# Two phases per 512 tokens in the mlp, and row maxima in visits of six banks, in a gated attention and mlp kernel

## The chip, the cores and the metric

The kernel runs on one core of a Trainium2 chip. The metric is the device time of one execution in microseconds (us), lower is better. The time of the kernel before is the median of three runs; the profile is of one further execution.

## What is computed

For 2048 tokens of width 448, a multi-head attention (16 heads of 28) and an mlp (pre-layernorm, 1792 hidden units, tanh gelu) are mixed by a gate per token. All is fp32.

```python
x = A_x                                              # [1, 2048, 448]
g = sigmoid((x * gate_w).sum(-1, keepdims=True))
q, k, v = split(x @ wqkv)                            # 16 heads of 28
a = softmax(q @ k.T * 28 ** -0.5) @ v                # per head
a = a.reshape(1, 2048, 448) @ wo
y = layernorm(x)                                     # over 448
b = gelu(y @ w1 + b1) @ w2 + b2                      # 448 -> 1792 -> 448
return g * a + (1 - g) * b
```

## The kernel before

**Split operands.** TensorE multiplies in fp32r, a rounded form of fp32. To keep the accuracy every operand is split in a rounded part (names with h: `w1h`, `yh`, `hh`, `khi`) and the rest (names with l: `w1l`, `yl`, `hl`, `klo`), and a product is the sum of three matmuls: high by high, high by low, low by high. The rounded part is written by ScalarE (`activation(..., Copy)`), the rest by a subtraction on GpSimd (POOL in the profile) or VectorE (DVE). The 448 rows of a contraction are four tiles of 128; the last holds 64 rows twice, high and low, and takes two matmuls. So a product over 448 takes 11 matmuls.

**Three stages, in order of the program.**

1. The projection (`qk_tile`, `v_tile`). For each chunk `c` of 512 tokens there are seven tiles of q and k, stored in DRAM as high and low part (`qk`), and four tiles of v with the gate's sum (`vs`). Eight PSUM banks are used in turn (`next_ps`). Beside it run the statistics of layernorm: `ln_stats` in chunk 1, `ln_rows` and `ln_turn` in chunk 2 (means and inverse deviations are transposed and stored as rows in `lns`), and the first layernorm, `ln_load` and `ln_apply`, in chunks 2 and 3. The weights of the first two column blocks are loaded in chunk 2 (`load_w`).

2. The mlp. The hidden units are 14 column blocks `f` of 128. `mlp1(c, f)` computes one block for 512 tokens in one PSUM bank, bank 0, with 11 matmuls (L419). ScalarE empties it twice with the gelu, once rounded (`hh`, L424) and once whole (`h`, L425), and GpSimd makes `hl` (L426). `mlp2(c, f)` adds the block's part to the output of four token tiles in banks 4 to 7, with three matmuls each (L432, L433, L435). The loop runs `mlp1` of a step and then `mlp2` of the step before, so 56 steps. At a chunk's end the four banks are copied (ScalarE; in the last chunk VectorE, L443) and stored in `gbs`. In the first chunk each step loads and splits the weights of the block after next: `load_w` with two staging buffers for w1 and two for w2. Layernorm of the next chunk (`ln_apply`, mostly on GpSimd) runs in steps 6 to 12 of a chunk, on double-buffered `yh`, `yl`.

3. The attention. 64 score units per 512 queries of four heads, five units at a time: three row-group matmuls per unit (L591), exponentials on ScalarE (L596), the product with v (L620), and every 512 queries a normalisation and the output projection (`finish`, `project`), added to the gated mlp output `acc`.

**Row maxima.** The softmax subtracts an approximate row maximum, taken over the product of the high parts of q and k alone. It is 64 matmuls for each of 16 groups of 512 queries and four heads (each contracts 28 rows in one of four row groups of the array, L313), a reduction on VectorE (L293 for one bank, L295 for two) and one closing transpose, 1040 items in all. The class `RowMax` makes them and `Filler` spreads them: in the mlp `filler.run` counts slots (one per mlp matmul) and, when at least `MG` items are due, makes a visit of `MG` matmuls in the banks from 1 on. `MLP_MAX` = 476 items are made in the mlp, from step `FS` on, and the rest in the attention.

```python
if self.max is not None and self.due(n) >= min(MG, self.upto - self.done) > 0:
    self.max.issue(1, min(MG, self.upto - self.done))
```

**Order.** TensorE's instructions stand in the order of the program in all stages. In the projection and the mlp the order on the other queues (ScalarE, VectorE, GpSimd, and SP, which issues the DMAs) comes from a scheduler; in the attention they too stand in program order. Each queue works strictly in its order.

## Time and profile before

| | |
|---|---|
| median of three runs | 1266.08 us (1265.72 to 1268.47) |
| profiled execution | 1261.53 us |
| its span, first to last instruction | 1259.7 us |
| mean granted TensorE clock | 0.981 |
| TensorE matmul busy | 1188.8 us (94%) |
| VectorE / ScalarE / GpSimd busy | 770.1 / 633.2 / 335.2 us |

How to read the rows in the next section. A row of stretches has the stretch, its length, then busy time and number of instructions of PE (TensorE matmul), PEld (its weight loads), DVE, ACT (ScalarE) and POOL, the granted clock (1.00 is full), the busy share of the DMA engines and GB/s. A row of groups has the line, engine, operation, output and inputs with shapes, the count, then busy us and mean ns of one, then the idle time of the engine just before them with what ended it. A row of a timeline has start, duration, engine, line and operation, and in brackets the idle time before it and what ended it. Matmuls are pipelined, so the durations of neighbours overlap.

### The profile page before, as it was taken

What the parts mean: (1) busy time and instruction counts of PE and PEld (TensorE: products, weight loads), DVE (VectorE), ACT (ScalarE), POOL (GpSimd) and SP (SyncE); (2) the same over time, 40 slices, a digit from 0 to 9 for tenths busy, and PEclk for the clock granted to TensorE, in tenths of its full rate; (3) what the DMA queues carried; (4) which work ended last, traced back from release to release, by engine and by line L of the source; (5) the groups of instructions that cost most, each with busy time, mean ns of one, the idle gap of its engine ahead of it and who ended that gap; (6) DMA issues with size and microseconds to landing.
All of it is one profiled execution on the core that took longest, in us unless ns stands there. A gap on an engine that the chain in (4) does not pass through costs nothing.

```text
span 1259.7 us, 19889 instructions
## 1 busy us (share of the span) xinstructions
PE 1188.8 (94%) x8133; PEld 690.9 (55%) x8133; DVE 770.1 (61%) x1118; ACT 633.2 (50%) x663; POOL 335.2 (27%) x361
## 2 busy tenths in 40 slices
PE   7998679899999999979999999999999999999997
PEld 5887556566666666654444444444444444444443
DVE  3543047677777777766666666666667666666503
ACT  5333531211222121227766776677667667766774
POOL 4014881611221111114424521122022202201220
PEclk9999889999999999989999999999999999999998
DMA  8986661200010000036310022010102100001001
GB/s 263 307 292 202 182 168 37 71 8 1 9 62 8 8 30 8 1 95 158 95 54 17 18 54 57 14 29 25 45 18 59 33 16 18 25 2 54 25 25 60
DMA packets 52328, 83.44 MB, mean 66 GB/s; under 512 B 8268, under 2 KB 28252, under 8 KB 51324
## 3 DMA queue, kind: packets, MB, share of 16 engines
q1 hardware_dynamic: 48044, 76.04, 20.1%
q0 software_dynamic: 4192, 6.12, 1.9%
q8 instruction: 64, 1.05, 0.4%
q14 instruction: 28, 0.23, 0.1%
HBM read 55.49 MB, written 26.49 MB: 65 GB/s over the span
## 4 chain that ended last, share of the span: by engine, by line
PE 80%; DMA 7%; POOL 5%; DVE 4%; issue 2%; SPq 1%; ACT 1%; DVEq 0%; POOLq 0%; ACTq 0%
PE bank L620 19%; PE bank L591 18%; PE bank L313 17%; PE bank L419 10%; PE bank L435 4%; PE bank L432 3%; PE bank L433 3%; PE bank L506 2%; DMA xraw<-in_xt 2%; DVE acc L509 2%; POOL vg L119 1%; PE bank L508 1%; PE bank L507 1%; POOL vg L118 1%; DMA r<-in_w 1%
## 5 line engine op out<-in xcount | busy, mean ns | idle before, releaser
L596 ACT ACTIVATE pt<-bank 128x1536 f32<-128x1536 f32 (+1 forms) x410 | 484.7, 1234 | 208.5 <-PE bank L591 208.5
L293 DVE TENSOR_REDUCE mx<-bank 128x1 f32<-128x512 f32 x712 | 473.0, 686 | 153.0 <-PE bank L313 143.4
L313 PE MATMUL bank<-khi,qd 28*128 28x512 f32 x1024 | 364.7, 490 | 29.1 <-DVE acc L509 20.8
L313 PEld LDWEIGHTS bank<-khi,qd 28*128 28x128 f32 x1024 | 143.5, 183 | 235.6 <-DVE mx L293 114.9
L620 PE MATMUL bank<-pt,vg 128*32 128x512 f32 x2048 | 262.9, 604 | 0.0
L295 DVE TENSOR_REDUCE mx<-bank 128x2 f32<-128x1024 f32 x156 | 190.9, 1224 | 114.5 <-PE bank L313 114.2
L591 PE MATMUL bank<-qh,khi 29*128 29x512 f32 x1024 | 218.2, 476 | 0.0
L424 ACT ACTIVATE hh<-bank,b1s 128x512 fp32r<-128x512 f32 x56 | 38.4, 686 | 295.8 <-PE bank L419 295.8
L591 PE MATMUL bank<-qh,klo 28*128 28x512 f32 x1024 | 184.7, 397 | 0.0
L591 PE MATMUL bank<-ql,khi 28*128 28x512 f32 x1024 | 180.9, 390 | 0.0
L419 PE MATMUL bank<-yh,w1f 128*128 128x512 f32 x448 | 153.2, 414 | 11.9 <-ACT h L425 11.9
L426 POOL TENSOR_TENSOR hl<-h,hh 128x512 fp32r<-128x512 f32 x56 | 71.8, 1283 | 281.4 <-ACT h L425 262.4
L509 DVE SCALAR_TENSOR_TENSOR acc<-bank,gate,acc 128x448 f32<-128x448 f32 x64 | 43.7, 684 | 105.7 <-PE bank L508 104.2
L591 PEld LDWEIGHTS bank<-qh,khi 29*128 29x128 f32 x1024 | 87.1, 183 | 37.7 <-ACT pt L596 32.3
L419 PEld LDWEIGHTS bank<-yh,w1f 128*128 128x128 f32 x448 | 83.4, 191 | 41.4 <-issue 14.4
L435 PE MATMUL bank<-w2h,hl 128*128 128x448 f32 x224 | 89.4, 399 | 14.0 <-POOL hl L426 14.0
L591 PEld LDWEIGHTS bank<-ql,khi 28*128 28x128 f32 x1024 | 94.2, 187 | 15.1
L591 PEld LDWEIGHTS bank<-qh,klo 28*128 28x128 f32 x1024 | 92.1, 186 | 5.3
L620 PEld LDWEIGHTS bank<-pt,vg 128*32 128x32 f32 x2048 | 45.8, 109 | 84.0 <-issue 83.2
L519 POOL DMA_DIRECT2D lt<-ob x15 | 10.8, 720 | 301.6 <-DVE ob L518 301.6
L432 PE MATMUL bank<-w2h,hh 128*128 128x448 f32 x224 | 86.4, 386 | 0.0
L433 PE MATMUL bank<-w2l,hh 128*128 128x448 f32 x224 | 82.9, 370 | 0.0
(97 smaller groups left out, 1097.2 us busy)
## 6 DMA issues: line engine op xcount, KB each, us to landing
qk<-hl SPq DMA_DIRECT2D x28, 512.0 KB
xraw<-in_xt SPq DMA_DIRECT2D x16, 256.0 KB
vs<-vt SPq DMA_DIRECT2D x16, 256.0 KB
vg<-in_xt SPq DMA_DIRECT2D x16, 256.0 KB
rc<-rls POOLq DMA_DIRECT2D x60, 64.0 KB, 2.2
bxr<-in_xk SPq DMA_DIRECT2D x8, 448.0 KB
r<-in_w SPq DMA_DIRECT2D x14, 256.0 KB
khi<-qk SPq DMA_DIRECT2D x16, 224.0 KB
```

The lines of the kernel that those rows point to most:

```text
L293: nc.vector.reduce_max(self.mx[:, c0:c0 + 1], bank[:, b0], axis=AX)
L295: nc.vector.reduce_max(self.mx[:, c0:c1 + 1:c1 - c0], bank[:, b0:b1 + 1], axis=AX)
L313: nc.tensor.matmul(bank[:, b], self.qds[self.n][r, i * P:(i + 1) * P], khi[self.n // NC][r, k * 512:(k + 1) * 512], start=True, stop=True)
L419: nc.tensor.matmul(ps, a, b, start=(i == 0), stop=(i == len(ops) - 1))
L426: nc.gpsimd.tensor_sub(hl[c, f], h, hh[c, f].bitcast(F32))
L432: nc.tensor.matmul(a, hh[c, f][:, sl], w2h[f], start=(f == 0), stop=False)
L433: nc.tensor.matmul(a, hh[c, f][:, sl], w2l[f], start=False, stop=False)
L435: nc.tensor.matmul(a, hl[c, f][:, sl], w2h[f], start=False, stop=(f == NF - 1))
L509: nc.vector.scalar_tensor_tensor(acc[:, tt], po, gate[:, tt:tt + 1], acc[:, tt], op0=OP.mult, op1=OP.add)
L591: nc.tensor.matmul(bank[:, u % U], a[r, k * P:(k + 1) * P], b[r], start=(i == 0), stop=(i == 2))
L596: nc.scalar.activation(t, bank[:, b:b + len(units)], AF.Exp, scale=SCALE)
L620: nc.tensor.matmul(pv[32 * j:32 * j + 32, :], vg[n // NC][:, k, 32 * j:32 * j + 32], probs.pop(4 * step + j), start=(k == 0), stop=(k == N ...
```

## The change

The mlp is done in two phases for each 512 tokens. First all 14 blocks of the first product are computed, in banks 0 and 1 in turn, and `hh` and `hl` of all of them are kept on chip. Then each of the four token tiles runs the whole second product, 42 matmuls into one bank (0 or 1), and is copied by ScalarE and stored. Six banks, 2 to 7, are now left for the row maxima, and a visit has six matmuls (`MG` = 6), from block `FS` = 4 of the first chunk on. The items of a group of four heads are taken by key quarter first, so that a key quarter can be replaced when all have used it.

All split weights of w1 and w2 stay on chip in one set. To make room, layernorm's output has one buffer, the row maxima read their keys from one buffer of 28 rows per head (`khr`, loaded in 16 DMAs of a quarter each), and the pool of the attention's keys, queries and v (`aq`) is opened after the last first product, in the memory that w1 and layernorm leave. w1, w2 and the x of layernorm share three staging buffers (`r`); w1 is loaded three blocks ahead, w2 in its own block. The low part of w2 is made by VectorE and all of layernorm's subtractions by GpSimd.

Layernorm's statistics come earlier: the first chunk's in projection chunk 0, with its own rows and transposes in chunk 1, and `ln_apply` of the first chunk in chunks 1 and 2. Three blocks of w1 are loaded in projection chunk 3.

```diff
+MLP_G = MLP_MAX // 260
-MG = 3
-FS = 5
+MG = 6
+FS = 4
...
+    khr = mpool.tile([P, S], F32R, name="khr", bufs=1)
...
+    def staged(width):
+        return my.tile([P, CH], F32, name="r", bufs=3)[:, :width]
+
+    def load_w1(f):
+        r = staged(CH)
+        nc.sync.dma_start(r, w1[f].rearrange("p t x -> p (t x)"))
...
+        nc.scalar.activation(w1h[f], r, AF.Copy)
+        nc.gpsimd.tensor_sub(w1l[f], r, w1h[f].bitcast(F32))
+
+    def load_w2(f):
+        r = staged(D)
+        nc.sync.dma_start(r, w2[f])
+        nc.scalar.activation(w2h[f], r, AF.Copy)
+        nc.vector.tensor_sub(w2l[f], r, w2h[f].bitcast(F32))
+
+    yh, yl = (my.tile([P, n, CH], F32R, name=f"y{n}") for n in (4, 3))
...
     def ln_apply(c, t):
...
+        x = staged(CH)
+        nc.sync.dma_start(x, xt[t, :, c * CH:(c + 1) * CH])
+        nc.gpsimd.tensor_sub(x, x, lnr[:, 0])
+        nc.gpsimd.tensor_mul(x, x, lnr[:, 1])
+        nc.scalar.activation(yh[:, t], x, AF.Copy)
         if t < 3:
-            eng.tensor_sub(yl[c][:, t], x, yh[c][:, t].bitcast(F32))
+            nc.gpsimd.tensor_sub(yl[:, t], x, yh[:, t].bitcast(F32))
...
+                if c == 0 and m in (3, 5):
+                    ln_stats(m // 4)
+                if c == 1 and m in (0, 2, 3):
+                    (ln_rows if m == 0 else ln_turn if m == 2 else lambda a, b: ln_load(0))(0, TPC)
+                if c == 1 and m >= 4 or c == 2 and m < 3:
+                    ln_stats(m - 2 if c == 1 else m + 5)
                 if c == 2 and m in (3, 5):
-                    load_w(m // 4, mw0, mw0, my)
...
+                    (ln_rows if m == 3 else ln_turn)(TPC, NT)
+                if c == 1 and m in (4, 6) or c == 2 and m in (0, 2):
+                    ln_apply(0, m // 2 - 2 if c == 1 else m // 2 + 2)
+                if c == 3 and m < 3:
+                    load_w1(m)
...
-            self.left = [[(i, k) for i in range(TPC) for k in range(4)] for _ in range(4)]
+            self.left = [[(i, k) for k in range(4) for i in range(TPC)] for _ in range(4)]
...
+                if c == NC - 1 and g < MLP_G and all(n != k for x in self.left for _, n in x):
+                    load_khr(g + 1, k)
...
-                self.max.issue(1, min(MG, self.upto - self.done))
+                self.max.issue(2, min(MG, self.upto - self.done))
...
+    def mlp1(f):
+
+        ps = bank[:, f % 2]
...
+    def mlp2(c, i):
+
+        sl = slice(i * P, (i + 1) * P)
+        a = bank[:, i % 2, :D]
+        for f in range(NF):
+            nc.tensor.matmul(a, hh[f][:, sl], w2h[f], start=(f == 0), stop=False)
+            nc.tensor.matmul(a, hh[f][:, sl], w2l[f], start=False, stop=False)
+            filler.run(2)
+            nc.tensor.matmul(a, hl[f][:, sl], w2h[f], start=False, stop=(f == NF - 1))
+            filler.run(1)
+        gb = mh.tile([P, CH], F32, name="h", bufs=2)[:, :D]
+        nc.scalar.activation(gb, a, AF.Copy)
+        nc.sync.dma_start(gbs[c * TPC + i], gb)
+
+    for c in range(NC):
+        for f in range(NF):
+            if c == 0 and f + 3 < NF:
+                load_w1(f + 3)
+            if c == 0 and f == 0:
+                for k in range(4):
+                    load_khr(0, k)
+            if c == 0 and f == FS:
                 filler.spread(nc.sync, MLP_MAX, (NC * NF - FS) * 23)
...
+            if c == 0:
+                load_w2(f)
+            mlp1(f)
+        if c == NC - 1:
+            m0.close()
+            aq = ctx.enter_context(tc.tile_pool(name="aq", bufs=1, side="right", reuse_waits="tile"))
+            load_khi(0)
+            load_klo(0)
+            load_q(0)
+            load_v(0)
+            load_qm(0)
+        else:
+            ln_load(c + 1)
+        for i in range(TPC):
+            if c + 1 < NC:
+                ln_apply(c + 1, i)
+            mlp2(c, i)
+    ml.close()
```

More of the change, by code (lines that the diff above doesn't have):

```diff
@@ L377, in load_klo @@
     def load_klo(g):
-        klo[g] = klob[g % 2]
+        klo[g] = aq.tile([P, S], F32R, name="klo", bufs=2)
         for j in range(4):
@@ L472 @@
-    m0.close()
+    ml = ExitStack()
+    mw2 = ml.enter_context(tc.tile_pool(name="mw2", bufs=1, reuse_waits="tile"))
+    mh = ml.enter_context(tc.tile_pool(name="mh", bufs=1, reuse_waits="tile"))
+    for f in range(NF):
+        w2h[f] = mw2.tile([P, D], F32R, name=f"w2h{f}")
+        w2l[f] = mw2.tile([P, D], F32R, name=f"w2l{f}")
+    hh, hl = {}, {}
+    for f in reversed(range(NF)):
+        hh[f] = mh.tile([P, CH], F32R, name=f"hh{f}")
+        hl[f] = mh.tile([P, CH], F32R, name=f"hl{f}")
@@ L488 @@
     ao = sb("ao", 2)
+    woh = aw.tile([P, NG, D], F32R, name="woh")
+    wol = aw.tile([P, NG, D], F32R, name="wol")
     spare = 0
@@ L499 @@
     b2b = aw.tile([P, D], F32, name="b2b")
-    for i in (1, 2):
-        qbuf.append((aw.tile([P, CH], F32R, name=f"qh{i}"), aw.tile([P, CH], F32R, name=f"ql{i}")))
     def project(g, tt, oh, ol):
```

178 lines of the change are left out of this document (48 added, 130 removed).

## The prediction

> **What bounds the kernel now.** I read the page first, then the busy time by stretches of the span, cut at the first matmul of the mlp (118.7 us), at the first score matmul of the attention (555.5 us) and at the disturbed places between.
>
> ```profile
> span 1259.7 us, 19889 instructions
> PE 1188.8 (94%) x8133; PEld 690.9 (55%) x8133; DVE 770.1 (61%) x1118; ACT 633.2 (50%) x663; POOL 335.2 (27%) x361
> ...
> 20.00:118.70 98.70, 97.92 (x442) 82.85 (x441) 43.69 (x90) 33.60 (x60) 18.61 (x14) 1.00 0.84 272
> 118.70:200.00 81.30, 59.75 (x244) 43.40 (x243) 23.92 (x30) 29.79 (x51) 60.73 (x50) 0.87 0.63 170
> ...
> 245.00:260.00 15.00, 10.63 (x37) 7.00 (x36) 6.45 (x8) 1.45 (x3) 6.47 (x6) 0.77 0.03 12
> 260.00:540.00 280.00, 279.63 (x1225) 186.45 (x1225) 213.34 (x244) 54.14 (x88) 56.08 (x46) 1.00 0.05 16
> ...
> 555.50:572.00 16.50, 9.91 (x67) 4.93 (x70) 7.44 (x15) 5.76 (x5) 2.29 (x2) 0.69 0.53 159
> ```
>
> TensorE (PE, the first pair of each row) fills every stage. From 260 to 540 us it is busy for 279.63 of 280 at clock 1.00, so no other engine's work is worth anything there, only what TensorE spends. It loses time in three places: the first 80 us of the mlp (59.75 of 81.30, clock 0.87), 245 to 260 us, and the change to the attention. The projection before 118.7 us is full (97.92 of 98.70).
>
> The mlp stage lasts 555.5 - 118.7 = 436.8 us. To split it I need the prices of its two kinds of work, from TensorE's timeline inside the full stretch.
>
> ```profile
> 302.52 0.39 PE L419 MATMUL bank<-yl,w1f 128*128 128x512 f32 x1
> 302.75 0.40 PE L419 MATMUL bank<-yh,w1f 128*128 128x512 f32 x1
> 303.08 0.50 PE L313 MATMUL bank<-khi,qd 28*128 28x512 f32 x3
> 303.51 0.73 PE L419 MATMUL bank<-yh,w1f 128*128 128x512 f32 x2
> 304.08 0.37 PE L432 MATMUL bank<-w2h,hh 128*128 128x448 f32 x1
> ...
> 304.69 0.36 PE L432 MATMUL bank<-w2h,hh 128*128 128x448 f32 x1
> ```
>
> The duration overlaps the next matmul, so starts are what counts. A matmul of the first product takes 0.23 us (302.52 to 302.75), one of the second 0.61 / 3 = 0.203 (304.08 to 304.69; the two between are left out). The mlp has 56 x 11 and 56 x 12 of them: 616 x 0.233 + 672 x 0.203 = 280 us. A visit of three row-maximum matmuls (L313) stands between: from 302.75 to 304.08 there are three mlp matmuls (0.70) and one visit, so the visit costs 1.33 - 0.70 = 0.63. The three start together (one row, x3); the array is given over to them and back, and that is most of the price.
>
> ```profile
> L295 DVE TENSOR_REDUCE mx<-bank 128x2 f32<-128x1024 f32 x116 | 141.9, 1224 | 51.8 <-PE bank L313 51.6
> ...
> L293 DVE TENSOR_REDUCE mx<-bank 128x1 f32<-128x512 f32 x117 | 79.9, 683 | 14.4 <-PE bank L313 14.3
> ...
> L435 PE MATMUL bank<-w2h,hl 128*128 128x448 f32 x152 | 59.5, 392 | 0.0
> ```
>
> These are the groups of 260 to 540 us. 152 / 4 = 38 column blocks of hidden units passed: 38 x (11 x 0.233 + 12 x 0.203) = 190 us. The other 90 belong to 117 visits (one single reduction each): 0.77 per visit, so 0.14 beside the bare 0.63 is waiting for banks and the closing of row chunks. For the stage: 476 / 3 = 159 visits x 0.77 = 122. What is left, 436.8 - 280 - 122 = 35 us, is stalls and the slow clock after them:
>
> ```profile
> L419 PE MATMUL bank<-yh,w1f 128*128 128x512 f32 x448 | 153.2, 414 | 11.9 <-ACT h L425 11.9
> ...
> L435 PE MATMUL bank<-w2h,hl 128*128 128x448 f32 x224 | 89.4, 399 | 14.0 <-POOL hl L426 14.0
> ```
>
> 26 of the 35 are two waits: the first product for the gelu that empties its only bank, the second for hl, which GpSimd makes in one queue behind weight splits and layernorm.
>
> **The change part by part.**
>
> *Visits of six.* 476 row matmuls stay before the attention, now in 80 visits. What the fourth to sixth cost is not in the mlp's rows; the attention has dense row-group work:
>
> ```profile
> 900.70 0.50 PE L313 MATMUL bank<-khi,qd 28*128 28x512 f32 x1 [0.78 <-DVE acc L509]
> 900.70 0.73 PE L591 MATMUL bank<-qh,khi 29*128 29x512 f32 x4
> 901.04 0.40 PE L591 MATMUL bank<-qh,klo 28*128 28x512 f32 x3
> 901.27 0.39 PE L591 MATMUL bank<-ql,khi 28*128 28x512 f32 x2
> ```
>
> Four matmuls of different row groups start together at 900.70, and the next wave follows the second after 0.23 (901.04 to 901.27). Six are a wave of four and one of two: 0.63 + 0.23 = 0.86. With 0.14 of waiting as today a visit is 1.0: 80 x 1.0 = 80 us against 122, 42 less. Bounds: 0.86 (69 us) if the waits go; 1.25 (100 us) if VectorE is late (first rival).
>
> *VectorE under it.*
>
> ```profile
> 303.62 1.23 DVE L295 TENSOR_REDUCE mx<-bank 128x2 f32<-128x1024 f32 x1 [0.65 <-PE bank L313]
> 304.76 0.68 DVE L293 TENSOR_REDUCE mx<-bank 128x1 f32<-128x512 f32 x1
> ```
>
> Reductions follow each other after 1.14. Three pairs end 0.54 + 2 x 1.14 + 1.23 = 4.05 us after the visit began. A slot is one mlp matmul; after the first four blocks 56 x 23 - 44 = 1244 are left, so a visit is due each 1244 / 476 x 6 = 15.7 slots: every 15.7 x 0.203 + 1.0 = 4.2 us in the second product, 4.65 in the first. It fits, by little; only the last two banks are in danger.
>
> *Two phases.* hh and hl of all 14 blocks stay on chip, so a token tile's second product asks for an hl made long before. The 14.0 us behind L426 go; nothing takes their place until hl of block 13, needed some 8 us after its matmuls (14 x 3 x 0.203). Layernorm of the next 512 tokens runs under the second product, 168 x 0.203 = 34 us and 11 visits, for 4 x 3 GpSimd passes of 1.27 = 15: hidden. Its yh is single now, so ScalarE's writes stand ahead of the last gelu and wait for block 13's reads; that costs one block, with the other bank's tile of 42 matmuls as cover.
>
> *The start of the mlp.*
>
> ```profile
> 122.02 0.63 ACT L120 ACTIVATE yh<-vg 128x512 fp32r<-128x512 f32 x1 [4.83 <-POOL vg L119]
> ...
> 127.42 0.54 ACT L188 ACTIVATE vt<-bank 128x448 f32<-128x448 f32 x1 [2.99 <-DMA vs<-vt]
> ...
> 128.96 1.28 ACT L424 ACT_TABLE_LOAD   x1
> ...
> 131.58 0.79 PE L419 MATMUL bank<-yh,w1f 128*128 128x512 f32 x1 [10.22 <-ACT h L425]
> ```
>
> TensorE waits 10.2 us for the first gelu. ScalarE is late there because layernorm's yh (4.83) and then the stores of v (2.99) block its queue. The change does that layernorm in the second projection chunk: 4.8 go. A second bank lets one more block (2.56) pass. Against it, one more pair of weight casts (0.63 + 0.57) and their DMAs stand ahead of the gelu, and the keys' load is 16 small transfers in SP's queue ahead of the last v stores. I take 10.2 - 4.8 - 2.6 + 2.5 = 5, and 1.5 for the clock: 6.5 (from 1, if nothing blocks, to 13, as now with its clock).
>
> *The first 512 tokens: a ring of three staging buffers.* w1 three blocks ahead, w2 at its own block, 28 loads in order.
>
> ```profile
> 129.85 0.33 SPq L90 DMA_DIRECT2D r<-in_w  x1
> ...
> 132.93 0.63 ACT L93 ACTIVATE w1f<-r 128x512 fp32r<-128x512 f32 x1 [0.42 <-DMA r<-in_w]
> ...
> 132.84 1.27 POOL L94 TENSOR_TENSOR w1f<-r,w1f 128x512 fp32r<-128x512 f32 x1
> ...
> 167.20 0.33 SPq L96 DMA_DIRECT2D r<-in_w  x1
> ...
> 171.74 0.58 ACT L99 ACTIVATE w2h<-r 128x448 fp32r<-128x448 f32 x1 [1.08 <-DMA r<-in_w]
> ```
>
> From issue to cast took 3.1 us at 129.85 and 4.5 at 167.20: 3.8. A w1 load holds its buffer for 3.8 + 0.63 + 1.27 and half an hl pass (0.6): 6.3; a w2 load, split on VectorE now, 3.8 + 0.57 + 0.7: 5.1; mean 5.7. 24 loads after the head start are 8 rounds, 46 us, and two blocks (6) follow the last. TensorE needs 14 x 2.56 + 7 visits = 43 for these blocks, so 46 + 6 - 43 = 9, less what the head start hides: 8 us in stalls of 1 to 3. Bounds: 0 (3.1 each time), 21 (4.5 and each time behind hl). The head of ScalarE's queue passes these waits to the gelus, and so to TensorE's two banks.
>
> *The change to the attention.*
>
> ```profile
> 559.91 0.62 DVE L443 COPY gb<-bank 128x448 f32<-128x448 f32 x1 [2.49 <-DMA gbs<-gb]
> ...
> 561.79 0.79 PE L313 MATMUL bank<-khi,qd 28*128 28x512 f32 x1 [3.56 <-DVE mx L293]
> ...
> 566.98 0.79 PE L313 MATMUL bank<-khi,qd 28*128 28x512 f32 x1 [2.26 <-DVE mx L293]
> ```
>
> VectorE's last copies of the mlp wait for stores and hold up the reductions: 3.56, and half clock after it (0.69). With the copies on ScalarE and spread over the last 40 us, that wait goes; the second (2.26, the output weights' load) stays, and the first exponential now waits for the last copy and its table. -6 (0 to -10). Keys, queries and v for the attention are loaded in the last second product, 34 us, on memory free by then: no cost.
>
> *The projection.* Two statistics loads of 448 KB come early in a stretch where the DMA share is 0.84, and the first layernorm moves here whole: its lnr (512 KB) and four x loads pass the projection's stores in SP's queue, and four writes of yh stand in ScalarE's queue ahead of evictions. Eight banks of 2.5 us cover what ScalarE is late; without that cover TensorE stops as at 131 us. GpSimd has room (18.61 busy of 98.70), and VectorE loses two passes per tile. +1.5 (0 to 6). In the attention the 564 other row matmuls and their slots are the same: 0.
>
> **Sum.** New mlp stage: 280 + 80 + 6.5 + 8 = 374.5, so -62; with -6 and +1.5, -66. The profiled execution was 1261.53 us (span 1259.7), which gives 1195; the median of the runs is 1266.08, 0.36% higher, so the forecast is 1200.
>
> **Rivals.**
> 1. *VectorE binds the visits.* For: 4.05 of 4.2 us, in the first 512 tokens also 14 splits of w2, and after a chunk's closing the pairs fall unevenly. Each visit then waits for the last reduction, 1.25 instead of 1.0: +20, 1220. Against: in the full stretch VectorE is busy for 213 of 280. The Trainium skill, TensorEngine Tiling (Array Packing), PSUM Bottleneck, says that packing the array speeds up the matmuls and not the emptying of the banks, which may become the limit. By it this rival is the main case. 0.15.
> 2. *The ring is slow*: 4.5 us a load and all behind hl, 21 instead of 8, and a longer start (13): +20, 1220. 0.12.
> 3. *No concurrency in the second wave*, or the exchange of the array is paid again: two visits' price, 1.53 for six. The 42 us go: 1242. Against: the attention's rows. That is the change not doing what it says. 0.05.
> 4. *Slower: the clock falls in the first 512 tokens.* If stalls of 1 to 3 us each hold TensorE at half clock, 14 x 2.56 = 36 us of matmuls take twice that; with loads of 8 us each (8 rounds x 4.2 = 34 more) the gain of 66 is gone: 1270. It decides from 7.5 us a load. For: the clock of 0.77 at 245 to 260 us. Against: from 260 to 540 us most visits hold a short wait, at 1.00; neither load shown took over 4.5. The Trainium skill, TensorE: Matmul & The Clock Gate, A second HAM failure mode, says that cycling through banks with small idle times between groups can make the clock swing; the stretch at 1.00 speaks against it here. 0.04.
>
> **How the numbers follow.** The main case has 0.64 and 1185 to 1225 for itself (down: waits in visits 11, ring 8, start 5, taken together as 15; up the same terms with 17, 13, 7 as some 25). With rivals 1 and 2 the range is 1183 to 1232; rivals 3, 4 and the tails stay out. Faster by over 0.2% (about what a measurement of this kernel tells from no change): the main case and rivals 1 to 3, 0.94, leaving 0.02 for a sum of mishaps at zero; slower 0.04.
>
> **What would show it.** Right: mlp stage of 370 to 385 us; six row matmuls in two starts 0.23 apart; no wait behind hl; first attention matmul near 495. Wrong: reductions back to back with TensorE waiting for them; clock below 0.9 after 125 us; waits for r of over 10 us in the first 512 tokens; a projection stage longer than 122.

## The result, and the profile after

The changed kernel takes 1196.95 us (median of four runs, 1192.24 to 1199.98) against 1265.9 us of the kernel before beside it: a ratio of 0.9453, 95% interval 0.9416 to 0.949. The forecast was 1200 (1183 to 1232). The profiled execution took 1192.24 us, with a span of 1190.5, where the prediction's sum gave 1195. So 69 us went, and 66 were forecast; but the terms are not that close one by one.

The page's first rows, its row of granted clock, and the busy time by stretches. I cut the span again at the first matmul of the mlp (132.1 us), at the first matmul of a second product (182.5) and at the first score matmul (490.5).

```profile
span 1190.5 us, 19884 instructions
PE 1134.6 (95%) x8136; PEld 679.7 (57%) x8136; DVE 764.2 (64%) x1081; ACT 636.0 (53%) x668; POOL 330.0 (28%) x355
...
PEclk9998999999999999899999999999999999999998
```

```profile
0.00:132.10 132.10, 114.54 (x488) 94.54 (x489) 45.72 (x101) 47.37 (x82) 34.19 (x37) 0.96 0.79 253
132.10:182.50 50.40, 44.53 (x198) 31.20 (x197) 35.02 (x36) 31.29 (x53) 33.25 (x26) 0.98 0.53 151
182.50:490.50 308.00, 307.89 (x1569) 232.51 (x1567) 253.98 (x263) 68.75 (x112) 99.54 (x81) 1.00 0.15 42
490.50:1190.50 700.00, 667.63 (x5885) 321.41 (x5884) 429.44 (x682) 488.61 (x421) 163.00 (x212) 0.99 0.16 43
```

TensorE did the same matmuls in 1134.6 us of busy time instead of 1188.8. The mlp lasts 358.4 us (50.4 + 308.0) instead of 436.8, and in its last 308 us TensorE is busy for 307.89 at clock 1.00. The projection is *longer*: 132.1 instead of 118.7, for three more small transposes (the trace holds 488 matmuls there, against 486). By stage:

| stage | before | after | measured | predicted |
|---|---|---|---|---|
| projection | 118.7 | 132.1 | +13.4 | +1.5 |
| mlp | 436.8 | 358.4 | -78.4 | -62 |
| attention to the end | 704.2 | 700.0 | -4.2 | -6 |
| span | 1259.7 | 1190.5 | -69.2 | -66 |

So two errors of about 12 and 16 us cancel, and it is luck that the total comes within 3 us of the sum. The experiments below go after both, and after the claim that the visits of six are where the gain comes from.

**The visits of six.** TensorE's timeline in a second product of the changed kernel:

```profile
303.70 0.37 PE L453 MATMUL bank<-w2h,hl 128*128 128x448 f32 x1
...
304.00 0.74 PE L308 MATMUL bank<-khr,qd 28*128 28x512 f32 x6
...
304.66 0.47 PE L450 MATMUL bank<-w2h,hh 128*128 128x448 f32 x1
...
304.97 0.36 PE L451 MATMUL bank<-w2l,hh 128*128 128x448 f32 x1
```

The six row matmuls stand in one row. Between the mlp's matmuls before and after them lie 0.96 us, of which 0.203 belong to the first: the gap of the visit is 0.76. By the starts of single matmuls in the trace the median over the 37 visits in second products is 0.76 and their mean 0.76 too, so hardly one of them waits. Four of the six start within 0.01 us, the last two 0.34 later. In the kernel before, the median gap of a visit of three is 0.53 in a first product, where all three start together, and 0.65 in a second, where the third starts 0.14 late.

The gap is not the whole price. The first mlp matmul behind a visit takes 0.10 us longer to the next start than the others: 0.31 instead of 0.203 here (304.66 to 304.97), and by the median 0.10 to 0.11 in both kernels, whatever the size of the visit. So a visit of three that waits for nothing costs 0.64 and one of six 0.85. The mean over all visits, waits included, is 0.78 with three before and 0.86 with six now: 0.14 of waiting before, 0.01 now.

The groups of 130 full us of the changed kernel (line, engine, operation, count, busy us and mean ns, then the idle time just before with what ended it):

```profile
L290 DVE TENSOR_REDUCE mx<-bank 128x2 f32<-128x1024 f32 x72 | 85.3, 1218 | 13.3 <-PE bank L308 13.3
L438 PE MATMUL bank<-y,w1f 128*128 128x512 f32 x243 | 59.9, 397 | 0.0
...
L453 PE MATMUL bank<-w2h,hl 128*128 128x448 f32 x76 | 28.8, 378 | 0.0
...
L288 DVE TENSOR_REDUCE mx<-bank 128x1 f32<-128x512 f32 x42 | 28.7, 683 | 6.9 <-PE bank L308 6.9
...
L308 PEld LDWEIGHTS bank<-khr,qd 28*128 28x128 f32 x189 | 10.9, 182 | 11.0 <-issue 4.4 <-DVE mx L288 3.5 <-DVE mx L290 2.3
```

With 226 matmuls of the second product the mlp's own work is 243 x 0.233 + 226 x 0.203 = 102.5 us. The other 27.5 belong to 189 / 6 = 31.5 visits: 0.87 for one, closings included, where the same sum gave 0.77 for a visit of *three* before. VectorE has 85.3 + 28.7 us of reductions in 130, and it waits for TensorE (13.3 and 6.9), not the other way round: the row matmuls' weight loads wait 5.8 us for a reduction.

**The projection.** The timeline around the two places where the layernorm's rows are transposed:

```profile
46.60 0.27 PE L207 MATMUL bank<-ident,mr 128*4 128x128 f32 x1
...
47.45 0.63 DVE L193 BATCH_NORM_STATS2 st<-bxr 128x6 f32<-128x448 f32 x1 [2.04 <-DMA bxr<-in_xk]
...
49.41 0.25 DVE L208 COPY rows<-bank 4x128 f32<-4x128 f32 x1
...
49.71 0.27 PE L207 MATMUL bank<-ident,mr 128*4 128x128 f32 x1 [2.83 <-DVE rows L208]
...
85.94 0.27 PE L207 MATMUL bank<-ident,mr 128*12 128x128 f32 x1
...
90.05 0.69 DVE L154 TENSOR_TENSOR xh<-xraw,xh 64x512 fp32r<-64x512 f32 x1 [1.08 <-ACT xh L150]
...
91.38 0.27 DVE L208 COPY rows<-bank 12x128 f32<-12x128 f32 x1
...
91.70 0.38 PE L207 MATMUL bank<-ident,mr 128*12 128x128 f32 x1 [5.49 <-DVE rows L208]
```

```profile
46.00:60.00 14.00, 11.16 (x44) 8.67 (x43) 6.41 (x14) 4.06 (x7) 0.00 (x0) 0.88 0.81 245
...
85.00:100.00 15.00, 9.51 (x38) 7.74 (x37) 5.45 (x11) 6.67 (x12) 3.21 (x4) 0.77 0.88 301
```

The changed `ln_turn` makes two transposes into one bank, with VectorE's copy between them. The second transpose waits for the copy of the first. At the first place that copy stands in VectorE's queue behind layernorm's statistics (L193), which wait 2.04 us for their load; at the second behind subtractions of `x` (the last is L154), which wait for ScalarE and the loads. TensorE, whose instructions stand in the order of the program, stops for 2.83 and 5.49 us, and runs at half clock for 3.4 us from 51.1 and 6.8 us from 88.6 (mean clock of the two stretches 0.88 and 0.77).

**The first 512 tokens and the change to the attention.** The waits from 132 to 184 us (who waits for whom: us in all, times, the longest), and a timeline of the change to the attention:

```profile
DVE w2l L100 <- ACT w2h L99: 14.5, 6, 4.4
...
ACT w2h L99 <- DMA r<-in_w: 7.8, 7, 2.1
PEld bank L308 <- DVE mx L290: 7.7, 9, 2.1
PE bank L308 <- DVE mx L290: 4.7, 5, 1.8
...
ACT w1f L93 <- DMA r<-in_w: 3.8, 6, 0.8
...
PE bank L438 <- ACT h L442: 1.1, 3, 0.6
```

```profile
491.23 1.28 ACT L578 ACT_TABLE_LOAD   x1
...
492.77 0.17 DVE L579 TENSOR_SCALAR gate<-gate 128x16 f32<-128x16 f32 x1 [1.03 <-ACT gate L578]
...
494.69 0.71 PE L308 MATMUL bank<-khr,qd 28*128 28x512 f32 x1 [1.98 <-DVE mx L288]
...
496.68 0.40 DVE L566 CAST woh<-ob 128x448 fp32r<-128x448 f32 x1 [2.04 <-DMA ob<-in_wo]
...
497.73 0.79 PE L308 MATMUL bank<-khr,qd 28*128 28x512 f32 x1 [0.18 <-DVE mx L288]
```

A staging buffer that comes late (7.8 us in seven waits) holds ScalarE's cast of w2. VectorE's queue waits for that cast to make w2l (14.5), reductions stand behind it, and the next visit's row matmuls wait for them (their weight loads 7.7, TensorE itself 4.7). At 490.5 the same pattern has another head: VectorE's steps of the gate wait for ScalarE's table load, the reductions stand behind them, and TensorE stops for 1.98 us until its bank is free. VectorE's next wait, 2.04 us for the output weights, costs TensorE only 0.18.

### The profile page after: what moved, and what is told of

Read it like the earlier page. It is cut to its first block, busy times and chain, and to the rows that moved or that the text cites. A ratio compares the mean times of both kernels' runs of the same rounds, so it can differ in the third digit from the quotient of the medians.

```text
span 1190.5 us, 19884 instructions
## 1 busy us (share of the span) xinstructions
PE 1134.6 (95%) x8136; PEld 679.7 (57%) x8136; DVE 764.2 (64%) x1081; ACT 636.0 (53%) x668; POOL 330.0 (28%) x355
## 4 chain that ended last, share of the span: by engine, by line
PE 83%; DMA 6%; DVE 4%; POOL 3%; issue 1%; ACT 1%; SPq 0%; DVEq 0%; POOLq 0%; ACTq 0%
PE bank L625 20%; PE bank L596 18%; PE bank L308 14%; PE bank L438 10%; PE bank L450 4%; PE bank L453 4%; PE bank L451 4%; PE bank L163 3%; PE bank L511 2%; DVE acc L514 2%; DMA r<-in_w 2%; DMA xraw<-in_xt 1%; PE bank L179 1%; PE bank L513 1%; PE bank L512 1%
## 5 line engine op out<-in xcount | busy, mean ns | idle before, releaser
L288 DVE TENSOR_REDUCE mx<-bank 128x1 f32<-128x512 f32 x624 | 412.6, 686 | 145.5 <-PE bank L308 135.3
L308 PE MATMUL bank<-khi,qd 28*128 28x512 f32 x512 | 241.8, 478 | 21.7 <-DVE acc L514 20.8
L290 DVE TENSOR_REDUCE mx<-bank 128x2 f32<-128x1024 f32 x200 | 235.2, 1218 | 37.7 <-PE bank L308 37.6
L308 PEld LDWEIGHTS bank<-khi,qd 28*128 28x128 f32 x512 | 92.3, 181 | 152.9 <-DVE mx L288 80.1
L596 PE MATMUL bank<-qh,khi 29*128 29x512 f32 x768 | 164.4, 477 | 0.3 <-ACT h L456 0.3
L438 PE MATMUL bank<-y,w1f 128*128 128x512 f32 x616 | 153.1, 399 | 1.1 <-ACT h L442 1.1
L596 PE MATMUL bank<-ql,khi 28*128 28x512 f32 x768 | 136.4, 392 | 0.0
L438 PEld LDWEIGHTS bank<-y,w1f 128*128 128x128 f32 x616 | 112.9, 188 | 37.0 <-issue 12.4
L308 PE MATMUL bank<-khr,qd 28*128 28x512 f32 x512 | 81.8, 467 | 7.0 <-DVE mx L290 4.7
L596 PEld LDWEIGHTS bank<-qh,khi 29*128 29x128 f32 x768 | 65.9, 183 | 31.9 <-ACT pt L601 26.4
```

What stands on the lines that cost most here:

```text
L288: nc.vector.reduce_max(self.mx[:, c0:c0 + 1], bank[:, b0], axis=AX)
L290: nc.vector.reduce_max(self.mx[:, c0:c1 + 1:c1 - c0], bank[:, b0:b1 + 1], axis=AX)
L308: nc.tensor.matmul(bank[:, b], self.qds[self.n][r, i * P:(i + 1) * P], khi[self.n // NC][r, k * 512:(k + 1) * 512], start=True, stop=True)
L438: nc.tensor.matmul(ps, a, b, start=(i == 0), stop=(i == len(ops) - 1))
L596: nc.tensor.matmul(bank[:, u % U], a[r, k * P:(k + 1) * P], b[r], start=(i == 0), stop=(i == 2))
```

## The experiments

Every ratio is to the kernel before, run beside it; "the change" is the changed kernel as given, 1196.95 us. Half clock at the start of the attention lasts from 0 to 17 us in the profiles, and the attention's length differs by up to 5 us between versions with the same attention (699.2 to 704.0 us with that of the change); smaller differences there are not read as effects.

### 1. Two banks for the two transposes

```diff
-            ps = next_ps()
             for n in range(2):
                 r = qw.tile([b - a, P], F32, name=f"rows{a}{n}")
+                ps = next_ps()
```

> Each of the two transposes of layernorm's rows takes a bank of its own instead of sharing one. Theory A (shared bank): the second transpose waits for VectorE's copy of the first, and that copy stands in VectorE's queue behind low parts of x that wait for x. Then the two idle times of 3.1 and 5.8 us at the transposes and most of the 10 us at half clock go: the projection ends near 121 to 123 us instead of 132, the time falls by 8 to 12 us. Theory B (the early loads fill the DMA queues and the projection starves whatever the bank): the idle time moves to the matmuls that wait for x, the projection still ends at 130 or later, the time changes by under 3 us. Theory C, on the start of the mlp: if the wait for the first gelu went only because the projection ended late, it comes back here as 3 to 8 us of idle time before the third block, and the gain is about 5.

Measured: 1187.1 us, ratio 0.9389 (0.936 to 0.9417), 10 less than the change. The same two stretches of time:

```profile
46.00:60.00 14.00, 14.00 (x65) 11.69 (x64) 7.17 (x16) 4.04 (x7) 0.00 (x0) 1.00 0.85 259
...
85.00:100.00 15.00, 15.00 (x71) 13.12 (x71) 5.35 (x11) 5.93 (x12) 2.58 (x2) 1.00 0.89 301
```

Both stops and their slow clock are gone, and the projection takes 122.8 us. Nothing of it came back at the start of the mlp, where TensorE's longest wait is 0.88 us. So 9.3 of the projection's 13.4 us are the shared bank. Single profiles differ by some us: the projection takes 132.1 to 135.2 us in the seven with the shared bank, 122.8 and 125.3 in the two with two banks. A smaller wait does appear later, 1.9 us at 184.8 us for the hl of block 13.

### 2 and 3. Visits of three and of four in the changed kernel

```diff
-MG = 6
+MG = 3
```

> The changed kernel with visits of three matmuls (banks 2 to 4). Wave account (a visit costs 0.63 us to give the array over and back with its first wave of up to four, and 0.23 for each further wave): 159 visits of 0.63 to 0.77 against 80 of 0.87, so 30 to 52 us slower, 1227 to 1249. If the gain came from the two phases and not from the visits' size: within 10 us of the changed kernel. If what a visit costs goes by its matmuls (0.145 each): no change.

> Visits of four matmuls, one wave. Wave account: 119 visits of 0.63, 75 us against 70, so 5 us slower (up to 17 with 0.10 of waiting in each). If every visit costs the same 0.87 whatever its size: 119 x 0.87 = 104, 34 us slower. If it goes by matmuls: no change.

Measured: 1246.8 us, ratio 0.9858 (0.9822 to 0.9895), with three; 1214.2, ratio 0.9607 (0.9581 to 0.9633), with four. The mlp after its first phase takes 357.5, 327.0 and 308.0 us for visits of three, four and six; the other stages are within 5 us of each other. So of the 69 us gained, 50 hang on visits of six instead of three; all the rest of the change, the projection's loss included, is worth 19. TensorE's timeline with visits of three, in a second product:

```profile
302.94 0.37 PE L453 MATMUL bank<-w2h,hl 128*128 128x448 f32 x1
...
303.24 0.85 PE L308 MATMUL bank<-khr,qd 28*128 28x512 f32 x3
...
303.60 0.18 PEld L308 LDWEIGHTS bank<-khr,qd 28*128 28x128 f32 x1 [0.17 <-DVE mx L288]
...
304.02 0.47 PE L450 MATMUL bank<-w2h,hh 128*128 128x448 f32 x1
```

Two of three start, the third waits for the reduction of its bank, and the gap of the visit is 1.08 - 0.203 = 0.88. Over all visits the medians of the gap are 0.53 (first product) and 0.67 (second) for three, 0.54 and 0.61 for four, 0.75 and 0.76 for six; with the 0.10 behind it a visit without a wait costs 0.64, 0.64 and 0.85. Up to four, row matmuls cost the same as three, since they start together; two more cost 0.21. And the short visits of the second product wait, the long ones do not.

The mean price, waits included, is 0.78 for three, 0.75 for four and 0.86 for six, and it accounts for the stretches: 142, 107 and 71 visits (427 to 430 row matmuls in the traces) come to some 111, 80 and 61 us, so 50 us more for three than for six and 19 for four, where 49.5 and 19.0 were measured. Of the 50 some 30 are the prices without waits (142 x 0.64 less 71 x 0.85) and some 20 the waits. Visits of four come out at the upper end of what was expected (17 us slower), for the same reason: they still wait.

An account by cycles fits that. A visit of n is due each 1244 / 476 x n mlp matmuls; in the second product that is 1244 / 476 x n x 0.203 plus the visit's price without waits, 2.23 us for three, 2.76 for four, 4.03 for six. With the prediction's reduction times (first start 0.54 after the visit's, a pair each 1.14, the last of a pair ending after 1.23, a single one 0.68) the reductions end 0.54 + 1.14 + 0.68 = 2.36, 0.54 + 1.14 + 1.23 = 2.91 and 4.05 us after the visit began. With three and four that is 0.13 and 0.15 too late for the last bank; with six it is 0.02, and the last two banks are asked for 0.34 later than the first. This is an argument from the account; what is shown is that the waits are there with three and four and not with six.

### 4. One more reduction in each visit of six

```diff
+    extra = const.tile([P, 1], F32, name="extra")
...
+            if n == MG:
+                nc.vector.reduce_max(extra, bank[:, first + n - 1], axis=AX)
```

The added reduction repeats the last bank's and its result is not used.

> VectorE reads the last bank of each full visit once more (one more reduction of 0.68 us per visit, its result unused). Cycle account: a visit waits only where the reductions of the visit before end later than the next visit's second wave. They end 4.05 us after the visit's start, 4.65 with the extra one; the next second wave comes 0.23 after a cycle of 4.07 us in the second product and of 4.5 in the first. So 0.35 us of waiting in each of some 40 visits of the second product, none in the first: 14 us slower, 5 to 20. If VectorE bound every visit already (the first rival of the prediction): 0.6 in each of 80, 48 slower. If it has slack in both (84% busy): under 3.

Measured: 1208.4 us, ratio 0.9561 (0.9523 to 0.96); the mlp after its first phase takes 320.4 us instead of 308.0. Groups of the same 130 us as above:

```profile
L291 DVE TENSOR_REDUCE mx<-bank 128x2 f32<-128x1024 f32 x72 | 85.2, 1218 | 5.0 <-PE bank L309 5.0
...
L333 DVE TENSOR_REDUCE extra<-bank 128x1 f32<-128x512 f32 x31 | 21.0, 678 | 0.0
```

VectorE got 0.68 us more per visit (21.0 / 31) and the mlp 12.4 us longer, 12.4 / 71 = 0.17 for each visit of that stretch. It waits for TensorE 5.0 us before the pairs, where it waited 13.3. Were VectorE the bound already, 71 x 0.68 = 48 us would have come. So there was slack of about half a microsecond per visit, and the change stands near the point where VectorE would decide, but on the good side of it. The first rival is refuted for this kernel.

### 5. Four staging buffers

```diff
-        return my.tile([P, CH], F32, name="r", bufs=3)[:, :width]
+        return my.tile([P, CH], F32, name="r", bufs=4)[:, :width]
```

> Four staging buffers instead of three. The first product of the first 512 tokens takes 50.4 us in the changed kernel (132.1 to 182.5) and its matmuls and visits make 42. If the ring of three paces it, four buffers cut a load's wait by a quarter: the stretch falls by 5 to 8 us, to 42 to 45, and the time by as much. Rival: what paces it is the order of ScalarE's queue (weight casts ahead of gelus) or the GpSimd queue, with buffers to spare: under 2 us.

Measured: 1200.8 us, ratio 0.9491 (0.9463 to 0.9519), no gain. From the first cast of w2 to the last, some 24 loads, it took 35.5 us instead of 39.9, yet the first 512 tokens' first product took 53.4 instead of 50.4. The timeline of its largest stop:

```profile
161.44 0.58 ACT L99 ACTIVATE w2h<-r 128x448 fp32r<-128x448 f32 x1 [3.52 <-DMA r<-in_w]
...
163.22 0.73 PE L438 MATMUL bank<-y,w1f 128*128 128x512 f32 x2 [3.06 <-ACT h L442]
```

One cast that waits 3.5 us for its load at the head of ScalarE's queue holds the gelu behind it, and through it TensorE. In this profile the longer ring moves that place and does not take it away. The 3 us more are hardly beyond what the stretch varies by between versions that leave its loads alone (48.5 to 51.9), and the two ratio intervals meet, so a loss isn't shown either.

### 6. No wait of VectorE for w2

```diff
+    zero = const.tile([P, D], F32, name="zero")
+    nc.vector.memset(zero, 0.0)
...
-        nc.vector.tensor_sub(w2l[f], r, w2h[f].bitcast(F32))
+        nc.vector.tensor_scalar(w2l[f], zero, 1.0, None, op0=OP.mult)
```

The low part of w2 is left out: VectorE writes zeros, and needs neither load nor cast.

> The low part of w2 is left out: VectorE writes zeros at its place instead of subtracting (the loads and ScalarE's casts of w2 stay), so VectorE waits for no weight. Theory: the first 512 tokens' first product (50.4 us, of which 42 are matmuls and visits) is held up because VectorE's queue waits 14.5 us for w2 casts and holds the reductions that free the visits' banks. Then the stretch falls to 43 to 45 and the time by 5 to 7 us. Rival: the casts in ScalarE's queue ahead of the gelus hold it up by themselves; then it stays at 48 to 50 and the waits turn from the reductions to the gelus.

Measured: 1192.8 us, ratio 0.9443 (0.9411 to 0.9476); the stretch takes 48.0 us instead of 50.4. The waits from 132 to 184 us now:

```profile
ACT w2h L101 <- DMA r<-in_w: 6.0, 7, 1.7
PEld bank L440 <- ACT h L444: 5.8, 5, 2.1
```

The wait of TensorE's weight loads for the reductions has turned into a wait for the gelus, 5.8 us, as the rival said. The interval meets that of the change, so a gain isn't shown. The stall has two ways from one cause, the load that a cast waits for: through VectorE to the visits, and through ScalarE to the gelus.

### 7. The gate's exponential before the end of the mlp

```diff
         for i in range(TPC):
             if c + 1 < NC:
                 ln_apply(c + 1, i)
+            elif i == 2:
+                tc.keep_in_program_order(nc.scalar.activation(gate, zall, AF.Exp, scale=-1.0))
+                nc.vector.tensor_scalar_add(gate, gate, 1.0)
...
```

The exponential and VectorE's three steps on it stand in the last 512 tokens' second product now, before its third token tile.

> The gate's exponential and its three small VectorE steps are placed in the last chunk's second product instead of between the mlp and the attention. Theory: in the changed kernel VectorE's queue waits there for ScalarE (copy, table load, gate: until 492.7 us), the first reductions of the attention come at 493.35, TensorE waits 2.0 us and then runs at half clock for 6.8 us. Then this wait goes, with most of the half clock: 4 to 5 us faster. Rival: the load of the output weights (VectorE waits 2.0 us for it at 496.7) takes its place as the next wait: under 2 us.

Measured: 1196.4 us, ratio 0.9466 (0.9427 to 0.9506), no gain. The timeline shows the next wait in VectorE's queue:

```profile
502.10 0.40 DVE L571 CAST woh<-ob 128x448 fp32r<-128x448 f32 x1 [3.90 <-DMA ob<-in_wo]
```

The output weights' load now holds VectorE, 3.90 us instead of 2.04, and TensorE stops for 1.97 us behind it. Half clock lasts 13.7 us where it was 6.8; the profiled run is the slowest of the four (1201.81 us).

### 8. The layernorm where the kernel before had it

```diff
...
-                if c == 0 and m in (3, 5):
-                    ln_stats(m // 4)
...
+                if c == 1 or (c == 2 and m == 0):
+                    ln_stats(m if c == 1 else 7)
+                if c == 2 and m == 2:
+                    ln_rows(0, NT)
+                if c == 2 and m == 4:
+                    ln_turn_all()
+                if c == 2 and m == 6:
+                    ln_load(0)
+                if c == 3 and m in (1, 2, 3, 4):
+                    ln_apply(0, m - 1)
```

`ln_turn_all` is one transpose of all rows into one bank, with one copy.

> The changed kernel with layernorm's statistics, rows, single transpose and first application at the places they had before (chunks 1 to 3 of the projection). Theory of the prediction (ScalarE's queue was blocked by layernorm at the mlp's start): the projection ends at 118 to 121 us and the wait for the first gelu comes back, 4 to 9 us of idle TensorE within the first three blocks, and half clock with it; the time is 1190 to 1197. Rival (the second bank and fewer loads at that point removed the wait, the place of layernorm did not matter): no idle time over 2 us there, the time is 12 us less than the changed kernel, 1182 to 1187.

Measured: 1187.2 us, ratio 0.9402 (0.9366 to 0.9437). The projection takes 119.3 us, and the wait for the first gelu is back. TensorE's and ScalarE's timelines at the start of the mlp:

```profile
120.80 0.55 ACT L181 ACTIVATE vt<-bank 128x448 f32<-128x448 f32 x1 [3.07 <-DMA vs<-vt]
...
123.79 0.58 ACT L99 ACTIVATE w2h<-r 128x448 fp32r<-128x448 f32 x1 [2.44 <-DMA r<-in_w]
...
129.79 2.50 PE L445 MATMUL bank<-y,w1f 128*128 128x512 f32 x5 [5.36 <-ACT h L449]
```

So doing the layernorm earlier costs 12.8 us of projection, 9.3 of which need not be (experiment 1), and the wait that it took from the start of the mlp is 5.36, near what the prediction had put on it (4.8). But the rows show another cause than the one that the prediction named: ScalarE waits for a store of v (3.07) and for weights (2.44), and its last write of yh is done at 104.9 us, 23 us before the first gelu. Nor is anything gained in all by an early layernorm: with two banks (experiment 1) it takes 1187.1 us, with the late one 1187.2, which is below the 1190 to 1197 that the theory had expected.

### 9. Experiments 1 and 7 and later output weights together

```diff
...
-                    if 2 <= k < 6:
-                        load_wo(k - 2)
+                    if 4 <= k < 12 and k % 2:
+                        split_wo(k // 2 - 2)
+                    if 2 <= k < 10 and k % 2 == 0:
+                        load_wo(k // 2 - 1)
```

The output weights are loaded at every second key step, and VectorE's split of one stands three key steps after its load.

> A bank for each transpose, the gate early, and each block of the output weights split three key steps after its load instead of right behind it. Theory: at the change to the attention two waits of VectorE's queue stand one behind the other, the gate's and the output weights'; taking the first alone gained nothing since the second came next. With both away the attention stage (690 us from its first score matmul in no wait, 700 to 705 in the runs so far) falls to 694 to 697 with no half clock at its start, and the time to 1179 to 1183, 4 to 8 less than with the transposes alone. Rival: a third wait (the exponentials' first buffers, queries of the next chunk) follows: 1185 to 1188.

Measured: 1183.9 us, ratio 0.9363 (0.9349 to 0.9377). At the start of the attention one stop of 1.13 us and 6.8 us of half clock remain; the attention takes 697.3 us. Against experiment 1 alone (0.936 to 0.9417) the two intervals meet, so what the later weights bring isn't shown to be more than nothing.

### 10. The layernorm in the middle of the projection

```diff
...
+                if c == 2 and m == 1:
+                    ln_rows(0, NT)
+                if c == 2 and m == 3:
+                    ln_turn_all()
+                if c == 2 and m == 4:
+                    ln_load(0)
+                if c == 2 and m == 6 or c == 3 and m < 3:
+                    ln_apply(0, (m + 1) % 7)
```

With it go experiment 9's gate and output weights and experiment 8's statistics and single transpose.

> The same two changes at the attention's start, and layernorm's statistics and its single transpose where they were before, its first application two tiles earlier (last tile of projection chunk 2, first three of chunk 3), so that ScalarE's last projection work has no layernorm behind it. Theory: the projection ends at 119 to 121 us and the wait at the mlp's start, 5.75 us in the run with the late layernorm, falls under 2: 1176 to 1181. Rival: that wait comes from the stores of v and the weights' casts ahead of the first gelu, not from layernorm: it stays at 4 to 6, 1180 to 1185.

Measured: 1183.0 us, ratio 0.9354 (0.9331 to 0.9377). The projection takes 119.1 us and the attention 694.7, without half clock at its start. But the wait at the start of the mlp is there, 6.43 us. Though the program asks for the first application two tiles earlier, the last write of yh is done at 104.9 us in both experiments, so this run doesn't vary what it was meant to. The waits of ScalarE at the start of the mlp:

```profile
121.48 0.55 ACT L181 ACTIVATE vt<-bank 128x448 f32<-128x448 f32 x1 [3.08 <-DMA vs<-vt]
...
124.68 0.58 ACT L99 ACTIVATE w2h<-r 128x448 fp32r<-128x448 f32 x1 [2.65 <-DMA r<-in_w]
...
126.98 0.63 ACT L93 ACTIVATE w1f<-r 128x512 fp32r<-128x512 f32 x1 [1.72 <-DMA r<-in_w]
```

ScalarE is held by a store of v and by the loads of the first weights, as in experiment 8; no write of yh stands near.

### 11. The keys of the row maxima asked for two blocks later

```diff
-            if c == 0 and f == 0:
+            if c == 0 and f == 2:
                 for k in range(4):
                     load_khr(0, k)
```

The rest is experiment 10's kernel.

> As the version with the layernorm in the middle and the output weights later (1183.0 us, start wait of 6.8 us and half clock for 6.8 us behind it), but the 16 key loads of the row maxima are asked for at block 2 of the mlp instead of block 0. In SP's queue the first three weight loads of the mlp now stand ahead of the last seven stores of q and k and of v instead of behind them; the last v stores are no earlier. Theory (SP's order: ScalarE's casts of w1 and w2, ahead of the first gelu, wait for loads that were issued late): the casts no longer wait at 124 to 128 us, the start wait falls to 1 to 3 us, the clock stays whole, and the time is 1173 to 1179. Rival 1 (the stores of v hold ScalarE's evictions, 3.1 us at 121.5, and the transfers are full): the wait stays at 4 to 7, 1181 to 1185. Rival 2: the first visits of row maxima, due at block 4, now wait for their keys; a gap of over 2 us near 140 us gives back what the start gained, 1180 to 1186.

Measured: 1187.0 us, ratio 0.9386 (0.9368 to 0.9403), not faster than experiment 10. TensorE's and ScalarE's timelines at the start of the mlp:

```profile
124.48 0.54 ACT L181 ACTIVATE vt<-bank 128x448 f32<-128x448 f32 x1 [3.11 <-DMA vs<-vt]
...
128.58 3.69 PE L445 MATMUL bank<-y,w1f 128*128 128x512 f32 x15 [3.70 <-ACT h L449]
```

The casts behind the store of v no longer wait, and the start wait falls from 6.43 to 3.70 us: 2.7 of it hung on SP's order, in which three weight loads now stand ahead of most of the key loads. The store of v still holds ScalarE, so the theory was half right at the start and wrong on the total. The gap near 140 us that the second rival named isn't there. The profile has other half-clock stretches instead (157.5, 184.8 and 488.6 us), the second after a wait of 1.89 us for block 13's hl. That they used up the gain is what the profile suggests; no run separates it.

## Why the prediction came out

**Visits: price right, waits wrong.** The prediction took a visit of six at 0.63 + 0.23 = 0.86 bare and 0.14 of waiting, and 80 of them for 80 us. Measured, the price without waits is 0.85 (0.64 for the first four and 0.21 for two more, though these start 0.34 after the first and not 0.23). The 0.63 of the one visit at 303.08 holds, too: its gap is 0.53, all three start together, and the other 0.10 is the matmul behind it (from 303.51 to 304.08 two matmuls take 0.57 us instead of 0.47). The step that failed is the 0.14 of waiting "as today". Of that, 0.01 is left; with closings a visit costs 0.87, and 80 x 0.87 = 70, which is the lower bound that the prediction gave for the case that the waits go. Its own account of VectorE, which said that visits of six just fit, was not put to the visits of three: there it gives 0.13 of lateness in the second product. A TensorE that is busy for 279.63 of 280 us shows nothing of such waits, as matmuls overlap in the profile.

**VectorE under it: right.** 4.05 of a cycle of 4.2 fitted, by little (the cycle is 4.03 without the waits, and the later start of the last two banks makes it fit). Experiment 4 shows the little: 0.68 us more per visit cost 0.17. The Trainium skill, TensorEngine Tiling (Array Packing), PSUM Bottleneck, was set against this: packing speeds up the matmuls and not the emptying of the banks. Its direction is seen here, since with 0.68 more, and with visits of three and four, the banks begin to decide; at the change's own size they don't (VectorE waits 20.2 us for TensorE in 130).

**Two phases: right in mechanism.** The 14.0 us of waits for hl are gone, and the stage came out at 358.4 us, below the 370 to 385 that would have shown the sum right, with the first score matmul at 490.5 and not 495. The one place that the prediction left open, the hl of block 13, costs nothing in the changed kernel, but 1.9 us in experiments 1 and 8 to 11, and 1.0 and 1.2 in 6 and 7.

**The start of the mlp: right sign, wrong size, reason not shown.** 6.5 us were forecast for it; TensorE's first wait in it is 0.24 us (at 137.5 us). The prediction let 4.8 of the old wait go with the writes of yh in ScalarE's queue. In experiments 8 and 10 a wait of 5.36 and 6.43 us comes back, while the last write of yh is done 23 us or more before the first gelu: there it is stores of v and weight loads that hold ScalarE. So the agreement of 5.36 with 4.8 is luck. Experiment 11 puts 2.7 of the 6.43 on SP's order, close to the 2.5 that the prediction charged for the key loads and the extra casts together. Why the stores are on time when the layernorm lies in the second and third chunk, and late when it lies at the end, wasn't separated: the change in transfers, GpSimd's queue and ScalarE's come together.

**The ring of three staging buffers: right number, by luck.** 8 us were forecast. The stretch took 50.4; 154 x 0.233 = 35.9 and seven visits of 0.87, 6.1, leave 8.4. But rounds took 39.9 / 8 = 5.0 us, not 5.7, and with 5.0 the prediction's own sum would give 40 + 6 - 43 = 3. The way of the stall is another, too: it was to go through ScalarE's queue to the gelus, and TensorE waits 1.1 us for gelus and 4.7 for reductions that stand behind VectorE's w2l. Experiments 5 and 6 show that it is neither the number of buffers nor VectorE alone; what is left, the order of ScalarE's queue, wasn't varied. By the total of ScalarE's waits for `r`, 7.8 + 3.8 = 11.6 us, the prediction's sign "waits for r of over 10 us" came true, without the loss that it was to tell of.

**The projection: the failed step.** +1.5 (0 to 6) was forecast, and +13.4 came, outside the bounds. The step costed DMAs, queues and evictions of the moved layernorm and took `ln_turn` for what it was before: it did not ask what the changed function does to TensorE. Its second transpose needs VectorE's copy of the first, and VectorE's queue at that place waits for loads. Experiment 1 gives 9.3 us of it back with one line. The prediction's own sign "a projection stage longer than 122" came true.

**The attention: close, and for much of the reason given.** -4.2 against -6. VectorE's waits for stores are gone, and TensorE's stop of 3.56 with them. The second stop, 2.26 for the output weights, did not stay as forecast: it is 0.18 now. In its place TensorE stops for 1.98 behind the gate's steps, which wait for a table load on ScalarE; the prediction had that load holding up the first exponential, not VectorE. Experiment 7 shows that taking it away uncovers the output weights again (1.97).

**Rivals.** The second wave costs 0.21 and not another visit's price, which ends rival 3. The clock in the first 512 tokens was 0.98, which ends rival 4: its stalls were short. The Trainium skill, TensorE: Matmul & The Clock Gate, A second HAM failure mode, has the clock swing under bank cycling with small idle times; with visits of three, four and six over 308 to 357 us the granted clock stayed at 1.00, so no run here shows it.

Two experiments ended below the change by 13 to 14 us (9 and 10: 1183.9 and 1183.0). Both leave a few us at the start of the mlp or of the attention.

## What to carry to other kernels

A small piece of work that is dropped into a stream of full-array matmuls is priced by its gaps, so count the interruptions first and make each as large as the engine behind it can follow; then look up where that engine's slack ends. Take the price up to where the stream is back at its pace, keep waits apart from it, and ask of each wait whether the change leaves it. When a helper function moves, read its body again for chains between engines: an instruction on the bound engine that needs an answer from another queue waits for everything that stands in that queue, as the second transposes did here (2.83 and 5.49 us).

## What the runs showed of the hardware

Row matmuls of three or four row groups, put into a first product, cost 0.64 us in all, and six 0.85; 0.10 of each falls on the first full-array matmul behind them. Half clock came in stretches of 3.4, 6.8, 10.2, 13.7 and 17.1 us, and the length of the stop alone doesn't tell whether it comes: a stop of 1.98 us at 492.7 was followed by 6.8 us of it in the changed kernel, one of 3.70 us at 124.9 in experiment 11 by none. Experiments 9, 10 and 11 have the same attention and the same stop near its start (1.13, 1.13 and 1.15 us), with 6.8, 0 and 10.2 us of half clock behind it: the attention took 697.3, 694.7 and 699.4 us, so here each us of half clock cost 0.4 to 0.5 us.
